# Loading x in 1 KB rows, writing the shuffle buffer in two parts and reading it in three: Fourier mixing and a three-way maxout layer on one Trainium2 core

## The chip, the core and the metric

The kernel runs on one core of a Trainium2 chip. The metric is the device time of one execution in microseconds (us). Five engines of the core take part, each with its own queue of instructions that it works through in order: PE (matmuls, with PEld for its weight loads), DVE (vector operations), ACT (activations and copies), POOL (table generation and the issue of some DMAs) and SP (the issue of other DMAs). Sixteen DMA engines move the data; SP's, ACT's and POOL's DMAs share them.

## What is computed

```python
X = np.fft.fft(np.fft.fft(x, axis=1), axis=2).real      # x: (8, 3072, 256), float32
t = X.reshape(24576, 256)
h = np.maximum(np.maximum(t @ w1, t @ w2), t @ w3)      # w1, w2, w3: (256, 768)
out = h @ w_out                                         # w_out: (768, 256)
```

## The kernel before

For each of the 8 batches the kernel first makes the Fourier mixing along the 3,072 rows, folded to its even and odd halves tE and tO ([128, 1536] each), and then runs the maxout layer on them. The transform along the 256 columns is folded into the weights once, at the start (gE, gO, gD, gw; `product`, `prep_first`, `prep_second`).

The mixing of one batch is done by class `Mix`, in steps that are called by letters in the plan:

- x is loaded by `load_x` as rows of 128 columns: row s of 96 in each of 32 blocks, with m the half of the columns, and h the block's front or its back, read from behind. Columns 0 to 127 go to partitions 0 to 63 of xt, columns 128 to 255 to partitions 64 to 127 of a second buffer xm. `mirror` (L125) and `mirror_first` (L129) copy that second half on DVE to xt in reversed order. Batch 0 is loaded by SP in float32 (x0) and cast by ACT and DVE; later batches are loaded by POOL, which casts to bfloat16.
- **s** (L349): a matmul over 128 partitions for 8 of the 49 rows s, copied to tb (s0 to s6).
- **y** (L363): tb is written to a buffer db in DRAM, in rows of 256 B.
- **z** (L370): db is read back as yb, with partitions and rows exchanged; four DMAs on SP.
- **x** (L377, L379): a small matmul for column 0 of x, which ACT copies straight into yb after z has landed.
- **k** (L388, L390): matmuls of yb with the tables te_tab and to_tab, for E and O and three groups g of 512 columns, copied to tE and tO by ACT. **end** (L395) does the middle row.

The maxout layer of a batch has 18 units (three blocks of six): `unit_plus` (L405, L406) gives one sign, ACT's relu (L419) and DVE's max (L420) take it to hp; `unit_minus` (L413) changes the accumulated sums to the other sign, which goes to hm. The second layer (`l2_block`: L429, L444, L452) follows one block later in pieces of ten between the units. Its sums become the tile ot on DVE (L457), which has six buffers; half of it is stored by SP (L469), half scattered by POOL (L462).

The order is written by hand. The dictionary `plan` says which steps of the next batch's mixing run in which unit: from batch 2 on, the s steps in units 1 to 4, y in 4, z in 6, x in 11, and the k steps in 12 to 17. `fetch` loads x of the batch after that in units 1, 3, 5 and 7, and `turn` mirrors it in 13 to 16. For mixings 1 and 2 the plan has lists of its own (`ahead0`, `ahead1`). Units above 17 lie in the next iteration.

Before the first unit the tables are made: POOL's iotas, DVE's range reduction, ACT's sines. The pool `gen` that holds them is closed ahead of the maxout layer, so that its space is used again by h_pool and others. load_w(0) waits for x's third chunk, load_w(1) for the first z. `warm_up` issues matmuls whose results are not used.

Of the kernel before, what the change touches and what calls it, by code (L numbers as in the profile page):

```python
# [9 lines left out]
FP32 = mybir.dt.float32  # L10
# [33 lines left out]
def kernel(  # L44
# [9 lines left out]
    nc = tc.nc  # L54
# [20 lines left out]
    xt = [consts.tile([128, 64 * 128], BF16, name=f"xt{i}", tag=f"xt{i}") for i in range(2)]  # L75
    xt = [t.rearrange("p (s f) -> p s f", f=128) for t in xt]
    xm_t = consts.tile([128, NS * 128], BF16, tag="xm")
    xm = xm_t.rearrange("p (s f) -> p s f", f=128)
    tb = consts.tile([128, 25 * 128], BF16, tag="tb")
    tbv = tb.rearrange("p (s f) -> p s f", f=128)  # L80
    yb = consts.tile([128, 2 * RI * 128], BF16, tag="yb")
    ybv = yb.rearrange("p (r e f) -> p r e f", e=2, f=128)
# [24 lines left out]
    def load_x(b, s0, s1, eng, dsts, after=None):  # L107

        rows = x[b].rearrange("(a s) (m f) -> m a s f", s=96, m=2)
        for m, dst in enumerate(dsts):  # L110
            if dst is None:
                continue
            for h in range(2):
                lo, hi = (s0, s1) if h == 0 else (max(s0, 1), min(s1, 48))
                src = rows[m]
                src = src[:, lo:hi, :] if h == 0 else src[:, 97 - hi:97 - lo, :][:, ::-1, :]
                p0 = 64 * m + 32 * h
                ld = eng.dma_start(out=dst[p0:p0 + 32, lo:hi, :], in_=src)
                if after is not None:
                    tc.add_manual_dep(ld.ins, after.ins.name, AFTER, reason="others first")  # L120
        return ld

    def mirror(b, s0, s1, src, fn):

        fn(out=xt[b % 2][64:128, s0:s1, 1:128], in_=src[64:128, s0:s1, 127:0:-1])  # L125

    def mirror_first(b, s0, s1, src, fn):

        fn(out=xt[b % 2][64:128, s0:s1, 0], in_=src[64:128, s0:s1, 0])  # L129

    gen_pool_cm = tc.tile_pool(name="gen", bufs=1)
    gen = gen_pool_cm.__enter__()
# [7 lines left out]
    FIRST = ((0, 16), (16, 32), (32, 40), (40, 49))  # L140
    x0_t = gen.tile([128, NS * 128], FP32, tag="x0")
    x0 = x0_t.rearrange("p (s f) -> p s f", f=128)
    for p0 in (32, 96):
        nc.vector.memset(x0[p0:p0 + 32, 0::48, :], 0.0)
    for c, (s0, s1) in enumerate(FIRST):
        ld = load_x(0, s0, s1, nc.sync, (x0, x0))
        if c == 2:
            third_chunk = ld
    nc.vector.memset(yb, 0.0)
    for i in range(2):  # L150
        nc.gpsimd.memset(xt[i][:, NS:64, 0], 0.0)
    nc.gpsimd.memset(xt[1][32:64, 0::48, :], 0.0)
    nc.gpsimd.memset(xm[96:128, 0::48, :], 0.0)
# [5 lines left out]
    iota(arv[:, :, 0:16], [[0, 4], [1, 16]], base=1)  # L159
    iota(arv[:, :, 16], [[0, 4]])  # L160
    dvec = gen.tile([128, 128], FP32, tag="dvec")
    iota(dvec, [[1, 128]])
    kvec = gen.tile([128, NHALF + 1], FP32, tag="kvec")
# [9 lines left out]

    half_pi = gen.tile([128, 1], FP32, tag="half_pi")
    nc.vector.memset(half_pi, 0.5 * math.pi)
    ang_o = gen.tile([128, 4 * RI], FP32, tag="ang_o")
# [36 lines left out]

    vm = gen.tile([128, 512], FP32, tag="vm")
# [18 lines left out]
    nc.scalar.activation(out=md_all, in_=vm, func=AX.Sin, scale=float(2.0 * math.pi / 256.0))  # L233
    nc.scalar.activation(out=nmd_all, in_=vm, func=AX.Sin, scale=float(-2.0 * math.pi / 256.0))

    act = nc.scalar.copy
    dve = nc.vector.tensor_copy

    def low_cast(s0, s1):
        act(out=xt[0][0:64, s0:s1, :], in_=x0[0:64, s0:s1, :])  # L240

# [16 lines left out]

    low_cast(*FIRST[0])
    mirror(0, *FIRST[0], x0, dve)  # L260
    mirror_first(0, *FIRST[0], x0, dve)
    angles(0, 512)
    low_cast(*FIRST[1])
    mirror(0, *FIRST[1], x0, dve)
    mirror_first(0, *FIRST[1], x0, dve)

# [10 lines left out]
    load_w(0, third_chunk)  # L277
# [3 lines left out]
    scal(dif, sgn, 1.0, ALU.subtract)  # L281

# [54 lines left out]
    class Mix:  # L337
# [7 lines left out]
        def s(self, k, pool=ps_f, evict=nc.scalar.copy):  # L345
            ps1 = pool.tile([128, 512], FP32, name="ps1", tag="ps")
            if k < 6:
                for hh in range(2):
                    nc.tensor.matmul(ps1, tab_at[hh], self.x[:, 8 * k + hh:8 * k + 8:2, :],  # L349
                                     start=(hh == 0), stop=(hh == 1))  # L350
                evict(out=tb[:, k * 512:(k + 1) * 512], in_=ps1)  # L351
            else:
                nc.tensor.matmul(ps1[:, 0:128], tab_at[0], self.x[:, 48, :],
                                 start=True, stop=True)
                evict(out=tbv[0:64, 24, :], in_=ps1[0:64, 0:128])

        def y(self, s0=0, s1=NS):
# [3 lines left out]
            for hh in range(2):  # L361
                n = (s1 - s0 + 1 - hh) // 2
                nc.sync.dma_start(out=dst[:, s0 + hh:s1:2, :],  # L363
                                  in_=tbv[hh * 64:hh * 64 + 64, s0 // 2:s0 // 2 + n, :])

        def z(self):
            for (a, z) in ((0, 48), (48, NS)):
                for cs in range(2):
                    q0, n = cs * 2 * RI * 128, (2 * RI - 4 * cs) * 128
                    last = nc.sync.dma_start(out=yb[cs * 64 + a:cs * 64 + z, 0:n],  # L370
                                             in_=self.db[a:z, q0:q0 + n])
            return last

        def x0(self, evict=nc.scalar.copy):
            psx = ps_f.tile([128, 512], FP32, name="psx", tag="ps")
            for cs in range(2):
                nc.tensor.matmul(psx[cs * 64:cs * 64 + 64, 0:RI], self.x[:, :, 0],  # L377
                                 tabx[:, cs * RI:(cs + 1) * RI], start=True, stop=True)
            evict(out=ybv[:, :, 1, 0], in_=psx[:, 0:RI])  # L379

        def k(self, which, g):

            special = {0: [(0, 0, 32)], 1: [(0, 0, 16), (16, 16, 16)], 2: [(16, 0, 32)]}[g]
            parts = special + [(5 * g + 1 + i, 32 + 96 * i, 96) for i in range(5)]
            tab = (te_tab, to_tab)[which]
            ps2 = ps_f.tile([128, 512], FP32, name="ps2", tag="ps")
            for (r, c0, wd) in parts:
                nc.tensor.matmul(ps2[:, c0:c0 + wd], ybv[:, (r - 1) % RI, which, :],  # L388
# [3 lines left out]
        def end(self):  # L392
            ps3 = ps_f.tile([128, 512], FP32, name="ps3", tag="ps")
            for which, tab in enumerate((te_tab, to_tab)):
                nc.tensor.matmul(ps3[:, which:which + 1], ybv[:, 16, which, :],  # L395
# [157 lines left out]
    warm_up(8)  # L553
    m.s(0, pool=ps_s, evict=dve)
    m.s(1, pool=ps_s)
    m.y(0, 16)
    warm_up(2)
    low_cast(*FIRST[2])
    mirror(0, *FIRST[2], x0, dve)
    mirror_first(0, *FIRST[2], x0, dve)  # L560
    m.s(2, pool=ps_s, evict=dve)
    m.s(3, pool=ps_s)
    m.y(16, 32)
    warm_up(2)
    low_cast(*FIRST[3])
    mirror(0, *FIRST[3], x0, dve)
    mirror_first(0, *FIRST[3], x0, dve)
    m.s(4, pool=ps_s, evict=dve)
    m.s(5, pool=ps_s)
    m.s(6, pool=ps_s, evict=dve)  # L570
    m.y(32, NS)
    y_first = m.z()
    tables(0, 512)
    angles(512, NHALF + 1)
    tables(512, NHALF + 1)

    for half in range(2):
        keep_product(product(0, half, 0, ps_f, "ps"), 0, half, 0, dve)
    for half in range(2):
        keep_product(product(1, half, 0, ps_s, "ps"), 1, half, 0, dve)  # L580
    m.x0()
    HALVES = ((0, 25), (25, NS))
    load_w(1, y_first)
    wld = nc.gpsimd.dma_start(out=wout_bf.rearrange("p (jc c) -> p jc c", jc=NJC),
                              in_=moe_w_out.rearrange("(jc p) c -> p jc c", jc=NJC))
    for (s0, s1) in HALVES:
        load_x(1, s0, s1, nc.gpsimd, (xt[1], xm))

    rows_f = gen.tile([128, 12 * B], FP32, tag="rows_f")
    rows_v = rows_f.rearrange("p (b r) -> p b r", r=12)  # L590
# [177 lines left out]
```

## Time and profile before

| | |
|---|---|
| median of 3 runs | 482.77 us (478.15 to 485.17) |
| the profiled execution | 484.2 us, of which 482.4 are the span of its instructions |
| mean granted clock of PE | 0.943 |
| iterations 2, 3, 4, 5 and 6, from end to end of a mixing (L395) | 52.78, 53.27, 54.61, 54.89, 47.45 us |
| PE's total wait for yb<-db in k (directly) | 18.5 us |
| DMA | 103,625 packets, 54.34 MB |

In the profile's rows a line begins with the engine and the line of the kernel; `out<-in` are tiles. Where a row ends in square brackets, they hold the time that the engine was idle ahead of it and what ended that. In the row of slices a digit is the busy share in tenths of a 40th of the span, or the granted share of PE's clock. "DMA share" is the mean busy share of the 16 DMA engines; it counts overlapping packets, so that it can exceed 1. A q behind an engine (SPq) marks its queue of DMA issues.

### The profile page before, as it was taken

The numbers are of one execution on the slowest core, as the hardware profiler recorded it, in microseconds if no ns is written. First come the engines' busy times: TensorE is split into PE (matmuls) and PEld (weight loads), VectorE is DVE, ScalarE is ACT, GpSimd is POOL, SyncE is SP. The second block draws the span as 40 slices with busy tenths as digits, with TensorE's granted clock in tenths as the row PEclk, the third lists the DMA queues.
The fourth block names the chain that finished last, engine by engine and source line by source line (L and its number), as shares of the span: only waits on it lengthen the run. The fifth ranks groups of instructions, "written<-read, shape, count | busy, mean of one in ns | idle before, by whom it ended". The sixth has DMA issues, their size and how long they took to land.

```text
span 482.4 us, 8139 instructions
## 1 busy us (share of the span) xinstructions
PE 417.0 (86%) x2756; PEld 254.5 (53%) x2756; DVE 296.2 (61%) x505; ACT 256.3 (53%) x470; POOL 172.9 (36%) x274
## 2 busy tenths in 40 slices
PE   0726979979984999799979999699969999999996
PEld 0312545546552666365646666365635656665665
DVE  6922784737553667385747666385736757667773
ACT  1741556546642765376535664366526665755550
POOL 3246134514450355133632456124621323222530
PEclk9966998989995999899998999799997999999999
DMA  9959316954594299625991399424981238222224
GB/s 164 182 110 169 33 19 92 237 100 86 79 190 104 69 134 167 137 76 89 179 173 48 82 144 168 107 84 78 177 171 42 84 83 176 64 78 67 74 67 123
DMA packets 103625, 54.34 MB, mean 113 GB/s; under 512 B 78600, under 2 KB 99856, under 8 KB 103192
## 3 DMA queue, kind: packets, MB, share of 16 engines
q0 software_dynamic: 54576, 24.70, 34.8%
q1 hardware_dynamic: 48848, 28.99, 27.1%
q8 instruction: 21, 0.34, 0.3%
q10 hardware_dynamic: 160, 0.13, 0.1%
q14 instruction: 20, 0.16, 0.1%
HBM read 34.73 MB, written 31.59 MB: 137 GB/s over the span
## 4 chain that ended last, share of the span: by engine, by line
PE 66%; DMA 23%; DVE 4%; ACT 3%; issue 2%; SPq 2%; POOL 1%; ACTq 0%; DVEq 0%
PE po L429 21%; DMA yb<-db 11%; PE pse L405 11%; PE pse L406 10%; PE pse L413 10%; DMA db<-tb 9%; PE ps L349 4%; PE po L452 3%; PE ps L388 2%; PE pl L444 2%; DMA wout_bf<-in_moe_w_out_dram 1%; DMA out_dram<-ot 1%; ACT stmp L419 1%; PE warm L550 1%; DVE hm L420 1%
## 5 line engine op out<-in xcount | busy, mean ns | idle before, releaser
L419 ACT ACTIVATE stmp<-pse 128x512 bf16<-128x512 f32 x288 | 169.8, 600 | 89.9 <-PE pse L406 69.5
L462 POOL DMA_INDIRECT out_dram<-ot,rows_m x92 | 107.5, 1168 | 268.6 <-DVE ot L457 249.5
L420 DVE TENSOR_TENSOR hp<-pse,stmp 128x512 bf16<-128x512 f32 x144 | 99.5, 691 | 137.9 <-ACT stmp L419 72.5
L405 PE MATMUL pse<-tE,gE 128*128 128x512 bf16 x288 | 112.3, 390 | 1.9 <-ACT stmp L419 1.3
L406 PE MATMUL pse<-tO,gO 128*128 128x512 bf16 x288 | 113.1, 393 | 0.1
L420 DVE TENSOR_TENSOR hm<-pse,stmp 128x512 bf16<-128x512 f32 x144 | 99.0, 688 | 11.4 <-ACT stmp L419 11.2
L413 PE MATMUL pse<-tO,gD 128*128 128x512 bf16 x288 | 88.7, 391 | 0.0
L429 PE MATMUL po<-wout_bf,hp 128*128 128x256 bf16 x576 | 87.3, 275 | 0.0
L429 PE MATMUL po<-wout_bf,hm 128*128 128x256 bf16 x576 | 81.2, 279 | 0.0
L429 PEld LDWEIGHTS <-hp 128*128 128x128 bf16 x576 | 57.0, 99 | 27.3 <-issue 1.1
L429 PEld LDWEIGHTS <-hm 128*128 128x128 bf16 x576 | 57.6, 100 | 18.7 <-issue 2.7
L457 DVE TENSOR_TENSOR ot<-po,even 128x512 f32<-128x512 f32 x92 | 62.8, 683 | 1.5 <-PE po L429 1.5
L413 PEld LDWEIGHTS <-gD 128*128 128x128 bf16 x288 | 28.3, 100 | 34.1 <-issue 3.2
L406 PEld LDWEIGHTS <-gO 128*128 128x128 bf16 x288 | 28.6, 99 | 26.4 <-issue 7.1
L405 PEld LDWEIGHTS <-gE 128*128 128x128 bf16 x288 | 28.7, 100 | 23.3 <-issue 2.6
L388 PE MATMUL ps<-te_tab,yb 128*128 128x96 bf16 (+2 forms) x152 | 11.6, 210 | 33.0 <-DMA yb<-db 18.5
L351 ACT CAST tb<-ps 128x512 bf16<-128x512 f32 x45 | 24.4, 588 | 25.1 <-PE ps L349 25.1
L388 PEld LDWEIGHTS <-yb 128*128 128x128 bf16 x304 | 17.7, 102 | 35.9 <-DMA yb<-db 28.5
L452 PE MATMUL po<-gw,tO 128*128 128x512 bf16 x92 | 36.0, 391 | 0.0
L349 PE MATMUL ps<-xt,tabz 128*128 128x512 bf16 x96 | 25.9, 390 | 4.2 <-DVE xt L129 2.4
L448 ACT COPY even<-pl 128x512 f32<-128x512 f32 x46 | 26.8, 583 | 0.8 <-PE pl L444 0.7
L379 ACT CAST yb<-psx 128x17 bf16<-128x17 f32 x8 | 1.9, 234 | 45.7 <-DMA yb<-db 30.2
(134 smaller groups left out, 271.3 us busy)
## 6 DMA issues: line engine op xcount, KB each, us to landing
out_dram<-ot SPq DMA_DIRECT2D x75, 96.0 KB, 1.9
yb<-db SPq DMA_DIRECT2D x8, 408.0 KB, 4.8
out_dram<-ot SPq DMA_DIRECT2D x48, 64.0 KB, 4.7
yb<-db SPq DMA_DIRECT2D x8, 360.0 KB
db<-tb SPq DMA_DIRECT2D x7, 400.0 KB, 7.7
xt<-in_x_dram POOLq DMA_DIRECT2D x14, 192.0 KB, 4.9
xm_t<-in_x_dram POOLq DMA_DIRECT2D x14, 192.0 KB, 8.6
db<-tb SPq DMA_DIRECT2D x7, 384.0 KB, 9.0
```

What stands on the lines that cost most here:

```text
L349: nc.tensor.matmul(ps1, tab_at[hh], self.x[:, 8 * k + hh:8 * k + 8:2, :], start=(hh == 0), stop=(hh == 1))
L388: nc.tensor.matmul(ps2[:, c0:c0 + wd], ybv[:, (r - 1) % RI, which, :], tab[:, g * 512 + c0:g * 512 + c0 + wd], start=True, stop=True)
L405: nc.tensor.matmul(pse[:, 0:n], gE[i][:, js], te, start=True, stop=False)
L406: nc.tensor.matmul(pse[:, 0:n], gO[i][:, js], to, start=False, stop=True)
L413: nc.tensor.matmul(pse, gD[i][:, js], to, start=False, stop=True, skip_group_check=True)
L419: nc.scalar.activation(out=stmp[:, 0:n], in_=pses[0][:, 0:n], func=AX.Relu)
L420: nc.vector.tensor_tensor(out=dst, in0=src3, in1=stmp[:, 0:n], op=ALU.max)
L429: nc.tensor.matmul(po, hcols(jc), wout_bf[:, jc * 256:(jc + 1) * 256], start=False, stop=(jc == NJC - 1), skip_group_check=True)
L448: nc.scalar.copy(out=even, in_=pl)
L452: nc.tensor.matmul(po, to[:, cp], gw[:, 256:768], start=True, stop=True)
L457: nc.vector.tensor_tensor(out=ot.rearrange("p (h c) -> p h c", h=2), in0=po.rearrange("p (h c) -> p h c", h=2), in1=lin.unsqueeze(1).to_br ...
L462: stored(nc.gpsimd.indirect_dma_start(out, bass.IndirectOffsetOnAxis(ap=rows_m[0:128 - lo, b * 12 + slot: b * 12 + slot + 1], axis=0), ot[ ...
```

## The change

- x is loaded as whole rows of 256 columns (1 KB in DRAM) to partitions 0 to 63 of a wider xt; DVE's mirror copies columns 255 to 129 from there to partitions 64 to 127, and the first column (128) with each chunk. The buffer xm is gone. Batch 0 is loaded in the same way by POOL, cast on the way; ACT's and DVE's casts are gone.
- y is in two parts, rows 0 to 23 after s2 and the rest after s6. z is in three parts of four DMAs, one for each group of k; the order of the rows in yb and in the tables' angles is changed to fit. At the start the last write's two DMAs are issued by SP and ACT.
- The small matmul for column 0 goes to a tile x0s without waiting for z; a copy c, on POOL (ACT for a part of batch 0), takes it from there into yb.
- The pool `gen` stays open to the end. rows_m is made earlier.
- The tables are made in three parts, the last in unit 0; warm-up matmuls are placed elsewhere (4, 8 and 12 in place of 8, 2 and 2); no product is made before unit 0; load_w(0) no longer waits, and load_w(1) waits for the first third of z.
- The plan: z in unit 7, c in 11, k in 13 to 17, x loads in 9 to 12, mirrors in 14 to 17; the two special lists alike.

```diff
+    def load_x(b, s0, s1, h):
+        rows = x[b].rearrange("(a s) d -> a s d", s=96)
+        lo, hi = (s0, s1) if h == 0 else (max(s0, 1), min(s1, 48))
+        src = rows[:, lo:hi, :] if h == 0 else rows[:, 97 - hi:97 - lo, :][:, ::-1, :]
+        return nc.gpsimd.dma_start(out=xt[b % 2][32 * h:32 * h + 32, lo:hi, :], in_=src)
+    def mirror(b, s0, s1):
+        t = xt[b % 2]
+        nc.vector.tensor_copy(out=t[64:128, s0:s1, 1:128], in_=t[0:64, s0:s1, 255:128:-1])
+        nc.vector.tensor_copy(out=t[64:128, s0:s1, 0], in_=t[0:64, s0:s1, 128])
-    gen_pool_cm = tc.tile_pool(name="gen", bufs=1)
+    gen = ctx.enter_context(tc.tile_pool(name="gen", bufs=1))
...
+        def z(self, parts=(0, 1, 2), engs=(nc.sync, nc.sync)):
+            spans = {0: ((0, 6, 0), (1, 6, 17)), 1: ((6, 12, 6), (6, 11, 22)),
+                     2: ((12, 17, 12), (12, 17, 27))}
+            for part in parts:
+                for cs in range(2):
+                    (i0, i1, c0) = spans[part][cs]
+                    c1 = c0 + i1 - i0
+                    for (a, z) in ((48, NS), (0, 48)):
+                        done.append(engs[cs].dma_start(
+                            out=yb[cs * 64 + a:cs * 64 + z, i0 * 256:i1 * 256],
+                            in_=self.db[a:z, c0 * 256:c1 * 256]))
...
-            evict(out=ybv[:, :, 1, 0], in_=psx[:, 0:RI])
+                nc.scalar.copy(out=x0s[cs * 64:cs * 64 + NS, :],
+                               in_=psx[cs * 64:cs * 64 + NS, 0:RI])
+        def c(self, i0=0, i1=RI, fn=nc.gpsimd.tensor_copy):
+            fn(out=ybv[:, i0:i1, 1, 0], in_=x0s[:, i0:i1])
...
+    for (u, fn) in ((0, lambda: tables(1024, NHALF + 1)), (0, lambda: m.c(6, RI)),
+                    (1, prep_some), (2, prep_some), (2, prep_some), (2, prep_some),
+                    (3, lambda: m.k(0, 1)), (3, prep_some), (4, lambda: m.k(1, 1)),
+                    (4, prep_some), (5, prep_some), (5, prep_some),
+                    (7, lambda: m.k(0, 2)), (8, lambda: m.k(1, 2)), (8, m.end)):
...
-        at(0, (6, 7, 8, 9)[ch], lambda ch=ch: turn(1, ch))
-        at(0, (10, 11, 13, 15)[ch], lambda ch=ch: fetch(2, ch))
+        at(0, (7, 8, 10, 11)[ch], lambda ch=ch: turn(1, ch))
+        at(0, (12, 13, 14, 15)[ch], lambda ch=ch: fetch(2, ch))
...
-            at(b - 2, (1, 3, 5, 7)[ch] + (4 if b == 3 else 0), lambda b=b, ch=ch: fetch(b, ch))
-            at(b - 2, (13, 14, 15, 16)[ch], lambda b=b, ch=ch: turn(b, ch))
+            at(b - 2, (9, 10, 11, 12)[ch], lambda b=b, ch=ch: fetch(b, ch))
+            at(b - 2, (14, 15, 16, 17)[ch], lambda b=b, ch=ch: turn(b, ch))
-    ahead0 = {9: ("s0", "s1"), 10: ("s2", "s3"), 11: ("s4", "s5"), 12: ("s6", "y"), 13: ("z",),
-              17: ("x", "kE0", "kO0"), 20: ("kE1", "kO1"), 24: ("kE2",), 25: ("kO2", "end")}
-    ahead1 = {5: ("s0", "s1"), 6: ("s2", "s3"), 7: ("s4", "s5"), 8: ("s6", "y"), 9: ("z",),
-              14: ("x", "kE0"), 15: ("kO0", "kE1"), 16: ("kO1", "kE2"), 17: ("kO2", "end")}
-    ahead = {1: ("s0", "s1"), 2: ("s2", "s3"), 3: ("s4", "s5"), 4: ("s6", "y"),
-             6: ("z",), 11: ("x",), 12: ("kE0",), 13: ("kO0",), 14: ("kE1",), 15: ("kO1",),
-             16: ("kE2",), 17: ("kO2", "end")}
+    late = {13: ("kE0",), 14: ("kO0", "kE1"), 15: ("kO1",), 16: ("kE2",), 17: ("kO2", "end")}
+    ahead0 = {8: ("s0", "s1"), 9: ("s2", "y0"), 11: ("s3", "s4"), 12: ("s5", "s6", "y1", "x"),
+              13: ("z",), 16: ("c",), 17: ("kE0", "kO0"), 20: ("kE1",), 21: ("kO1",),
+              24: ("kE2",), 25: ("kO2", "end")}
+    ahead1 = {3: ("s0", "s1"), 4: ("s2", "y0", "s3"), 5: ("s4", "s5"), 6: ("s6", "y1", "x"),
+              9: ("z",), 12: ("c",), **late}
+    ahead = {1: ("s0", "s1"), 2: ("s2", "y0", "s3"), 3: ("s4", "s5"), 4: ("s6", "y1", "x"),
+             7: ("z",), 11: ("c",), **late}
```

## The prediction

> **What bounds the kernel now.** I read the page's busy times first, then its row of slices, to see whether one engine is full and where it is not.
>
> ```profile
> PE 417.0 (86%) x2756; PEld 254.5 (53%) x2756; DVE 296.2 (61%) x505; ACT 256.3 (53%) x470; POOL 172.9 (36%) x274
> PE   0726979979984999799979999699969999999996
> PEclk9966998989995999899998999799997999999999
> DMA  9959316954594299625991399424981238222224
> ```
>
> PE is the engine to fill: 417.0 us of 482.4. It is full in the last third and has a dent about every 53 us before that, with DMA digits near 9 just ahead of each dent. Second view, the waits, all engines, to see what those 65 idle us wait for:
>
> ```profile
> ACT yb L379 <- DMA yb<-db: 30.2, 5, 10.0
> ...
> PE ps L388 <- DMA yb<-db: 18.5, 6, 8.2
> ...
> PE ps L388 <- ACT yb L379: 11.2, 3, 4.4
> ...
> PE psg L289 <- DMA w_bf<-in_moe_w_dram: 5.0, 2, 4.2
> ...
> PE ps L349 <- DVE xt L129: 2.4, 1, 2.4
> ```
>
> The dents are the read of the shuffled buffer (yb<-db): the k step's matmuls wait for it, directly or through the small copy L379, which stands in ACT's queue. Third view, the stretches between two ends of a mix (L395): iterations 2, 5 and 6 of the loop over batches (columns: us, then busy us and count of PE, PEld, DVE, ACT, POOL; clock; DMA share; GB/s).
>
> ```profile
> 162.02:214.80 52.78, 49.17 (x335) 30.33 (x333) 33.69 (x55) 30.24 (x57) 21.11 (x32) 0.97 0.67 121
> ...
> 322.68:377.57 54.89, 50.20 (x336) 30.75 (x334) 33.62 (x55) 30.23 (x57) 21.04 (x32) 0.94 0.63 117
> 377.57:425.02 47.45, 47.45 (x336) 29.90 (x333) 31.08 (x50) 30.48 (x57) 14.28 (x24) 1.00 0.43 103
> ```
>
> Iteration 6 does the same PE work (336 matmuls), loads no x, and takes 47.45 us with PE busy throughout. So it is a measured model of an iteration without the wait. The timeline tells what differs (write L363, read L370, copy L379, of iterations 4 and 6):
>
> ```profile
> 284.75 3.52 SPq L363 DMA_DIRECT2D db<-tb  x2
> ...
> 294.58 1.48 SPq L370 DMA_DIRECT2D yb<-db  x2
> ...
> 305.89 0.23 ACT L379 CAST yb<-psx 128x17 bf16<-128x17 f32 x1 [7.02 <-DMA out_dram<-ot]
> ...
> 306.17 0.66 PE L388 MATMUL ps<-te_tab,yb 128*128 128x32 bf16 x6 [3.89 <-ACT yb L379]
> ...
> 394.25 1.70 SPq L363 DMA_DIRECT2D db<-tb  x2
> ...
> 401.39 1.39 SPq L370 DMA_DIRECT2D yb<-db  x4
> ...
> 409.33 0.23 ACT L379 CAST yb<-psx 128x17 bf16<-128x17 f32 x1 [0.96 <-PE psx L377]
> ```
>
> In iteration 4 two x loads are issued at 284.87 and two at 293.61, beside write and read; 21.1 us pass from the write's issue to the copy, in iteration 6 at most 15. PE idles 3.89 us and restarts with 512-column matmuls of 0.60 instead of 0.38 us, so a dent costs more than its idle time. Last, the start:
>
> ```profile
> 32.97 0.21 PE L388 MATMUL ps<-te_tab,yb 128*128 128x32 bf16 x1 [6.00 <-DMA yb<-db]
> ...
> 42.73 0.73 POOL L118 DMA_DIRECT2D xm_t<-in_x_dram  x1 [1.05 <-DMA wout_bf<-in_moe_w_out_dram]
> ...
> 44.58 0.60 ACT L419 ACTIVATE stmp<-pse 128x512 bf16<-128x512 f32 x1 [9.24 <-POOL rows_f L137]
> ```
>
> The first relu waits until 44.58, since its tile lies where the table pool was and rows_f, last of that pool, stands on POOL behind all of batch 1's x loads.
>
> **The change part by part.** All is summed against the profiled execution: 484.2 us, span 482.4 and 1.8 around it. It lies 1.4 above the median 482.77.
>
> *x in 1 KB rows.* 6,144 rows of 512 B per batch become 3,072 of 1 KB. No row shows this load. Nearest: at 430 to 470 us only 1 KB stores run, DMA share 0.24 at 69 GB/s, which is 0.24 x 16 / 67.4 rows per us = 57 ns a row and engine; 512 B rows at 0 to 10 us (0.96, 158 GB/s) take 50 ns. A batch's x costs 3,072 x 57 / 16 = 10.9 us of all engines, at most twice 50, which is the 19 us of now. I take 11, from the row of equal size. Issues on POOL go from eight to four a batch (0.78 us each), hidden in POOL's idle time.
>
> *Mirror.* Same elements, 0.56 us for 64x1524, now from partitions 0-63 to 64-127: no row shows DVE shifting partitions. Lower bound 0.56, upper the rate of the two-tensor fp32 add (0.69 us for 512, 1.23 for 1,025, so 1.75 for 1,524): +1.2 us x 4 a batch on a DVE with 14 us to spare per iteration; I take 0.56. The first column costs three copies more, under 0.28 each (L129). Both lie under PE's work; without that cover they would cost at most 5.5 us an iteration.
>
> *Write in two, read in three.* SP issues two writes more (0.7 each) and eight reads more (0.31 each): 4 us an iteration. Behind them in SP's queue stand only stores, whose six buffers cover half an iteration. POOL's last x load at the start waited for the load eight before it, so I expect a ninth read to wait for the first; that delays the last third, needed last. SP already shows 25.3 us of stores waiting for yb<-db at no visible cost.
>
> *Order.* From batch 2 on: first write after s2, second at unit 4, read at unit 7 (was 6), E matmuls at 13 (was 12), x loads at 9 to 12 (were 1 to 7), mirrors at 14 to 17. Write and read then meet only stores, as in iteration 6: read issued 7.1 us after the write, landed within 7.6 more. From unit 7 to 13 there are about 6 x 2.4 = 14 us. The small copy leaves ACT: psx goes to x0s without waiting, and the column copy c waits on POOL at unit 11, behind it one x load and scatters. kE0 already waited for the copy's write, so it will wait for c; c needs all twelve reads, 9.6 us after the first. Fits. Iterations 2 to 5: 52.78 + 53.27 + 54.61 + 54.89 - 4 x 47.45 = 25.8 us; x loads and mirrors remain in them, so I take 25 (bounds 12 and 25.8).
>
> *Iteration 1.* From psx to the mix's end 19.54 us pass for three units and all k groups; iteration 6 does six units with them in 16.04, so three fewer at 2.24 make 9.3. Excess 10.2 (8.25 idle, the rest low clock; its write took 15.8 us among x loads). x now follows the read; I take 9.5 (5 to 10.2).
>
> *Iteration 0.* Gone: PE's 2.4 us wait for a mirror and 3.1 (2.36 and 0.76) for the read. New: s1 stands in the same unit as its mirror chunk, s4 too (about 1.2 each); three products in unit 2 instead of spread (0 to 2, I take 0.6); the read still meets batch 2's x loads, units 12 to 15 (I take 2 of the 3.1). 5.5 - 2.4 - 0.6 - 2 = 0.5 (-4 to 5).
>
> *Start.* Gone: 16 loads on SP, ACT's casts (1.9 us for 64x2048), the wait for rows_f. Added on POOL ahead of its tables: eight loads, 6.2 us. The last write is issued near 24 us, as now: rows_m's dozen small DVE operations (0.15 each) come ahead of the last mirror, ACT's casts go. Its DMAs are small, and the first third of the read lands some 2 us before the whole (33.0). But 24 warm-up matmuls (12 now) and tables up to 1,024 lie before it, so I count no gain to k. After k, PE did about 3.7 us of use between 35.3 and 44.94 (one product, one unit, half a product), so 6 were lost; those go. Tables of the last 513 columns (3.2 us for 1,025, so 1.6) now press on ACT in unit 0: -1, the rest under PE's work. Warm clock: +0.5. Sum 5.5 (-1 to 10).
>
> *On the page's other side.* The trace has a mirror against a POOL scatter: 1.95 us where 0.56 is usual, the scatter 2.68 where 1.04 is:
>
> ```profile
> 66.16 2.68 POOL L462 DMA_INDIRECT out_dram<-ot,rows_m  x1 [14.93 <-DVE xt L125]
> ...
> 67.25 1.95 DVE L125 COPY xt<-xm_t 64x1524 bf16<-64x1524 bf16 x1
> ```
>
> If the eight first loads, now on POOL, suffer likewise (2.6 instead of 0.78 us), they take 21 us, the last chunk's s6 comes near 27 instead of 23, and the start loses 4 where I count +5.5. The Trainium skill (SBUF — State Buffer, "SBUF: two separate sides") speaks for this: POOL writes the descriptors of its loads through a port that two-port DVE instructions lock. By that rule the start is A below; the pair above agrees with it.
>
> Sum: 25 + 9.5 + 0.5 + 5.5 = 40.5; 484.2 - 40.5 = 443.7, less the 1.4: 442.3, say 442.
>
> **The rivals.** *A, the start is not shorter* (above): start -4, else as forecast: 484.2 - 31 - 1.4 = 452. For it: that pair, and a POOL order in which kvec's tables and the weights stand behind x. Against: but for one memset of 1.87 us, DVE's early instructions are short (0.06 to 0.5).
>
> *B, half of the wait stays.* Twelve reads in one queue, c behind POOL's scatters (each waiting for ot), E matmuls behind c: if c runs after unit 13, PE waits as now. Half of 25 + 9.5 kept, start as forecast: 442 + 17 = 459, up to 473 if the start fails too (9.5) and iteration 0 loses 4. For it: L379's waits of 6 to 10 us. Against: iteration 6.
>
> *C, slower: the mirrors wait for x.* Fetched at units 9 to 12, used from 14; the last chunk's load has four units, about 11 us. The mirror stands in DVE's in-order queue; behind it hp and hm, then PE. Slowest class of x load now: 13.5 us to landing. Five iterations fetch so; the gain of 40.5 is eaten when each waits 8.1 us, a landing 19 us after issue. At 22 it is 5 x 11 = 55 lost: 497. For it: all x now goes to 64 partitions, at the busiest point behind the read. Against: half as many rows, and x loads of partitions 0-63 landed in 4 to 5.5 us, those of 64-127 in 6 to 13.5. The Trainium skill (SBUF — State Buffer, "Door 1: The DMA port swizzle") says partitions 0-63 reach half the DMA ports that 0-127 reach, about 218 GB/s; as an estimate from that page, 1.57 MB of bf16 then needs 7.2 us, below the 11 from rows, so it would not bind. No run here shows it alone.
>
> **How the numbers follow.** Forecast 0.62, own range 432 (all upper bounds: 25.8 + 10.2 + 5 + 10 = 51) to 454. A 0.16, B 0.14, C 0.08. About 2% (9.7 us) is what a measurement of this kernel can tell from no change. Faster by over 2% (under 473): forecast, A, most of B: 0.88; within 2%: 0.05; slower: 0.07. Range 430 to 466: it takes in A and B's middle, leaves out B's end and C.
>
> **What would show it.** Right: stretches between mix ends near 47.5 us in iterations 2 to 5, no L388 wait for yb or c above 1 us, clock 1.00 there; first relu near 36 us. Wrong: DVE idle before the mirror with the x load as releaser (C), POOL's c waiting past unit 13 (B), first s6 past 25 us (A). A mirror row above 1 us would put the bound on DVE.

## The result and the profile after

The changed kernel takes 450.88 us (median of 4 runs, 450.28 to 454.19); the kernel before, beside it, 483.97 (478.15 to 487.45). The ratio is 0.937, interval 0.927 to 0.947: faster. The forecast, 442, is 8.9 us too low; its range (430 to 466) holds the time. The medians in this document are over all runs of a kernel, while the ratios leave out the runs that came out in a slower state of the chip: five of e5's ten, one of e3's four, and two of the thirteen of the kernel before beside e5 and e7 to e9. The profiled execution took 451.0 us with a span of 449.2, 33.2 less than the span of before.

The page of the kernel after, busy times and slices:

```profile
PE 406.6 (91%) x2768; PEld 250.8 (56%) x2768; DVE 296.1 (66%) x527; ACT 255.2 (57%) x481; POOL 155.1 (35%) x263
...
PE   1488889599987999999998999999999999999994
...
PEclk9999999869998999999999999999999999999999
DMA  7849246912496236943397257924693354312323
```

PE's row is 8 or 9 from slice 14 to the last but one; the dents that are left after the start lie in slices 8 and 13 (11.2 us each, so near 85 and 140 us: iterations 0 and 1). PE is busy for 406.6 instead of 417.0 us for 12 instructions more: PEclk, at 5 to 8 around each dent before, now stays at 9 behind slice 13. The stretches of the kernel after between two ends of a mix say the same (iterations 1, 2, 4 and 6; columns as in the prediction):

```profile
117.95:150.01 32.06, 27.40 (x199) 17.04 (x196) 19.52 (x33) 16.46 (x30) 12.33 (x19) 0.95 0.62 133
150.01:198.16 48.15, 47.59 (x337) 29.88 (x334) 33.47 (x56) 30.53 (x58) 17.60 (x29) 1.00 0.59 132
...
247.24:295.11 47.87, 47.57 (x336) 29.87 (x333) 33.73 (x57) 30.52 (x58) 17.56 (x29) 1.00 0.60 134
...
342.81:390.23 47.42, 47.42 (x336) 29.89 (x333) 32.09 (x52) 30.52 (x58) 14.44 (x25) 1.00 0.38 103
```

Set against the terms of the sum, from the ends of the mixes in both traces:

| part | before | after | gained | predicted |
|---|---|---|---|---|
| start and iteration 0 (to the second mix's end) | 123.94 | 117.95 | 6.0 | 5.5 + 0.5 |
| iteration 1 | 38.08 | 32.06 | 6.0 | 9.5 |
| iterations 2 to 5 | 215.55 | 192.80 | 22.75 | 25 |
| iteration 6 | 47.45 | 47.42 | 0 | 0 |
| rest, after the last mix | 57.38 | 58.97 | -1.6 | 0 |

The column of gains adds up to 33.2. The waits of the k step that are left stand in iterations 0 (2.71 and 3.53 us) and 1 (1.30 and 3.36). The timeline of the kernel after at the k step of iteration 1 (start, duration, instruction; in brackets the engine's idle time and what ended it):

```profile
133.76 0.40 PE L395 MATMUL ps<-te_tab,yb 128*128 128x96 bf16 x6 [1.30 <-DMA yb<-db]
...
139.61 0.26 POOL L385 COPY yb<-x0s 128x17 bf16<-128x17 bf16 x1 [8.84 <-DMA out_dram<-ot]
139.92 0.40 PE L395 MATMUL ps<-to_tab,yb 128*128 128x96 bf16 x6 [3.36 <-POOL yb L385]
```

Two things are to be seen. kE0 (te_tab) runs at 133.76, six us before the column copy c (L385): it does not wait for c, against what the prediction says. kO0 (to_tab) does; by the code c writes only the half of yb that kO0 reads. And c itself stood on POOL for 8.84 us. The line puts that down to a store of ot, but c reads no ot; what it needs, by the code, is the read.

### The profile page after: what moved, and what is told of

It is laid out like the page before. It is cut to its first block, busy times and chain, and to the rows that moved or that the text cites. A ratio compares the mean times of both kernels' runs of the same rounds, so it can differ in the third digit from the quotient of the medians.

```text
span 449.2 us, 8328 instructions
## 1 busy us (share of the span) xinstructions
PE 406.6 (91%) x2768; PEld 250.8 (56%) x2768; DVE 296.1 (66%) x527; ACT 255.2 (57%) x481; POOL 155.1 (35%) x263
## 3 DMA queue, kind: packets, MB, share of 16 engines
q0 software_dynamic: 23856, 26.28, 29.7%
## 4 chain that ended last, share of the span: by engine, by line
PE 70%; DMA 11%; DVE 7%; issue 4%; ACT 3%; SPq 2%; POOL 1%; DVEq 0%; ACTq 0%; POOLq 0%
PE po L436 22%; PE pse L412 12%; PE pse L420 11%; PE pse L413 11%; DMA yb<-db 5%; PE ps L344 5%; PE po L459 3%; DMA xt<-in_x_dram 3%; DMA out_dram<-ot 3%; ACT stmp L426 2%; DVE hm L427 2%; PE pl L451 2%; PE ps L395 2%; SPq L476 1%; DVE ot L464 1%
## 5 line engine op out<-in xcount | busy, mean ns | idle before, releaser
L469 POOL DMA_INDIRECT out_dram<-ot,rows_m x92 | 105.4, 1146 | 234.2 <-DVE ot L464 219.2
L412 PE MATMUL pse<-tE,gE 128*128 128x512 bf16 x288 | 110.0, 382 | 3.1 <-DVE hm L427 2.4
L413 PE MATMUL pse<-tO,gO 128*128 128x512 bf16 x288 | 110.0, 382 | 0.1
L420 PE MATMUL pse<-tO,gD 128*128 128x512 bf16 x288 | 86.6, 382 | 0.0
L436 PE MATMUL po<-wout_bf,hm 128*128 128x256 bf16 x576 | 78.6, 273 | 0.0
L344 PE MATMUL ps<-xt,tabz 128*128 128x512 bf16 x96 | 27.5, 403 | 18.7 <-DVE xt L117 17.8
L346 ACT CAST tb<-ps 128x512 bf16<-128x512 f32 x47 | 25.9, 588 | 30.5 <-PE ps L344 30.5
L397 ACT CAST tO<-ps 128x512 bf16<-128x512 f32 x24 | 14.1, 586 | 24.0 <-PE ps L395 12.9
L116 DVE COPY xt<-xt 64x1524 bf16<-64x1524 bf16 (+4 forms) x32 | 19.1, 596 | 9.4 <-DMA xt<-in_x_dram 5.6
L397 ACT CAST tE<-ps 128x512 bf16<-128x512 f32 x24 | 14.1, 587 | 19.4 <-PE ps L395 19.4
```

The lines of the kernel that those rows point to most:

```text
L397: nc.scalar.copy(out=(self.tE, self.tO)[which][:, g * 512:(g + 1) * 512], in_=ps2)
L412: nc.tensor.matmul(pse[:, 0:n], gE[i][:, js], te, start=True, stop=False)
L413: nc.tensor.matmul(pse[:, 0:n], gO[i][:, js], to, start=False, stop=True)
L420: nc.tensor.matmul(pse, gD[i][:, js], to, start=False, stop=True, skip_group_check=True)
L436: nc.tensor.matmul(po, hcols(jc), wout_bf[:, jc * 256:(jc + 1) * 256], start=False, stop=(jc == NJC - 1), skip_group_check=True)
L469: stored(nc.gpsimd.indirect_dma_start(out, bass.IndirectOffsetOnAxis(ap=rows_m[0:128 - lo, b * 12 + slot: b * 12 + slot + 1], axis=0), ot[ ...
```

## The experiments

Twelve kernels were run. The prediction's reason, theory 1 in what follows, is the place of the x loads: they were beside write and read, and now stand behind the read. Its rivals: that the copy for column 0 left ACT's queue (4a where the theories are split), that the read was cut into parts, that the rows are longer. Iterations are measured from mix end to mix end; iteration 0 starts at the end of the first mix, and their lengths are those of the one profiled execution of each kernel. They carry noise: e6, whose edit lies ahead of unit 0, differs from the kernel before by 3.9 us in iterations 2 to 5 (211.64 to 215.55), so differences of that size in the last column say nothing. By 2%, e5, e6 and e8 are the same as the kernel before, e10 is unclear, and the others are faster.

| label | median | ratio to before, interval | iterations 0; 1; 2 to 5 together |
|---|---|---|---|
| kernel after | 450.88 | 0.937 (0.927-0.947) | 61.19; 32.06; 192.80 |
| e1_x_early | 446.62 | 0.922 (0.917-0.926) | 58.71; 29.50; 192.14 |
| e2_read_whole | 446.45 | 0.921 (0.917-0.925) | 57.28; 29.99; 190.40 |
| e3_x_behind_0_1 | 440.33 | 0.908 (0.903-0.913) | 52.56; 28.72; 194.02 |
| e4_half_rows | 451.63 | 0.933 (0.928-0.937) | 58.48; 31.08; 193.14 |
| e5_before_order | 485.33 | 0.994 (0.989-1.000) | 63.05; 39.87; 212.09 |
| e7_early_half_rows | 446.81 | 0.923 (0.916-0.929) | 60.26; 31.38; 190.76 |
| e8_early_c_on_act | 477.23 | 0.987 (0.981-0.994) | 58.88; 34.02; 214.26 |
| e9_behind_whole | 437.85 | 0.903 (0.897-0.909) | 52.87; 30.13; 190.70 |
| e10_before_c_pool | 479.78 | 0.987 (0.980-0.994) | 59.84; 39.36; 206.63 |
| e11_before_c_pool_k13 | 465.97 | 0.958 (0.951-0.965) | 60.07; 39.97; 194.51 |
| e6_before_rows | 479.54 | 0.988 (0.980-0.995) | 60.47; 38.20; 211.64 |
| e12_start | 435.76 | 0.897 (0.890-0.903) | 52.56; 30.21; 190.55 |

### The first four: one part of the change undone, or carried further

**e1_x_early**: the kernel after, its x loads at the units of before.

```diff
-        at(0, (12, 13, 14, 15)[ch], lambda ch=ch: fetch(2, ch))
+        at(0, (10, 11, 13, 15)[ch], lambda ch=ch: fetch(2, ch))
...
-            at(b - 2, (9, 10, 11, 12)[ch], lambda b=b, ch=ch: fetch(b, ch))
+            at(b - 2, (1, 3, 5, 7)[ch] + (4 if b == 3 else 0), lambda b=b, ch=ch: fetch(b, ch))
```

> The changed kernel with the x loads put back to their old units (1, 3, 5, 7; 5, 7, 9, 11 for batch 3; 10, 11, 13, 15 for batch 2), all else as changed. Theory 1 (the old dents came from x loads beside the write and the read, and the new order takes them away): dents return in iterations 2 to 5, which go from 48.2 us in the mean to 50 to 52, and the time from 451 to 459 to 467; less than before the change, since x now has half as many rows. Theory 2 (splitting the read and taking the small copy off ACT removed the dents, the order of x does not matter): within 3 us of 451.

No dent came back in iterations 2 to 5: they take 192.14 us, 0.7 less than in the kernel after, and the whole is 4.3 us faster, a little below what theory 2 allowed and far from the 459 to 467 of theory 1. x stands beside write and read again, and the read lands late again: in these iterations c stands 5.2 to 7.1 us for it on POOL, against 0.9, 6.2, 1.7 and 1.3 us in the kernel after. The copy c in iteration 4, of the kernel after and then of e1 (the releasers named are again not what c needs):

```profile
281.70 0.26 POOL L385 COPY yb<-x0s 128x17 bf16<-128x17 bf16 x1 [1.74 <-ACT even L455]
...
279.65 0.26 POOL L385 COPY yb<-x0s 128x17 bf16<-128x17 bf16 x1 [5.38 <-DMA out_dram<-ot]
```

PE does not notice. So the new order does bring the read forward, but the dents stay away without it. In iteration 1 the kernel after is even slower than this one (32.06 to 29.50): there x now stands at units 9 to 12 and the read at 9.

**e2_read_whole**: the kernel after, each read in six DMAs over the whole range instead of twelve.

```diff
-            for part in parts:
-                for cs in range(2):
-                    (i0, i1, c0) = spans[part][cs]
...
+            for (cs, i0, i1, c0) in ((0, 0, 17, 0), (1, 1, 11, 17), (1, 12, 17, 27)):
+                c1 = c0 + i1 - i0
```

> The changed kernel with the read in six DMAs of whole ranges in place of twelve in three parts; the write stays in two. Theory 1 (the dents left in iterations 0 and 1 are x loads beside the read): these dents stay at 2 to 4 us each, kE0 waits longer at the start and in iteration 0 since no first third lands early: 451 to 455. Theory 3 (they come from twelve reads in a queue that lets only eight be under way, so that the last ones and the column copy come late): the dents shrink, 445 to 448.

The cut into thirds does not carry the gain: without it iterations 3 to 5 take 47.42 us each, as iteration 6, and in iterations 2 to 5 c finds the read landed, where it stood up to 6.2 us in the kernel after. This is what theory 3 said of twelve reads. Only batch 0 loses by it: its k waits until 34.72 us instead of 30.91, and mix 0 ends 4.0 us later. The later iterations win that back and 4.4 us more.

**e3_x_behind_0_1**: the kernel after, x of batch 2 at units 15 to 18 of iteration 0 and of batch 3 at 11 to 14 of iteration 1, its mirrors one unit later.

```diff
-        at(0, (12, 13, 14, 15)[ch], lambda ch=ch: fetch(2, ch))
+        at(0, (15, 16, 17, 18)[ch], lambda ch=ch: fetch(2, ch))
...
-            at(b - 2, (9, 10, 11, 12)[ch], lambda b=b, ch=ch: fetch(b, ch))
-            at(b - 2, (14, 15, 16, 17)[ch], lambda b=b, ch=ch: turn(b, ch))
+            at(b - 2, (9, 10, 11, 12)[ch] + (2 if b == 3 else 0), lambda b=b, ch=ch: fetch(b, ch))
+            at(b - 2, (14, 15, 16, 17)[ch] + (1 if b == 3 else 0), lambda b=b, ch=ch: turn(b, ch))
```

> The changed kernel with batch 2's x loads at units 15 to 18 of iteration 0 (was 12 to 15), batch 3's at 11 to 14 of iteration 1 (was 9 to 12) and batch 3's mirrors one unit later. Theory 1 (x beside the read makes the dents left in iterations 0 and 1, 6.2 and 4.7 us of idle PE and the low clock behind them): they go, 439 to 444. Theory 3 (twelve reads through eight places): they stay, 449 to 453. If the mirrors of batches 2 and 3 now wait for x, PE idles before s0 and the time is above 451.

10.6 us by the medians, and iterations 0 and 1 are 8.6 and 3.3 shorter. Here the order does count: in these two iterations the kernel after issues x at the read's own units, close ahead of the read's use. The timeline of this kernel at the first k step of iteration 0, where the kernel after waits 2.71 us for the read and 3.53 for c:

```profile
83.21 0.39 PE L395 MATMUL ps<-te_tab,yb 128*128 128x96 bf16 x6
...
83.90 0.26 POOL L385 COPY yb<-x0s 128x17 bf16<-128x17 bf16 x1 [0.17 <-DMA yb<-db]
...
84.22 0.40 PE L395 MATMUL ps<-to_tab,yb 128*128 128x96 bf16 x6 [0.62 <-POOL yb L385]
84.38 0.54 POOL L111 DMA_DIRECT2D xt<-in_x_dram  x1 [0.22 <-issue]
```

The last x load is issued behind c, and PE's idle time ahead of kO0 falls to 0.62 us. In iteration 1 waits of 1.23 and 1.77 us stay.

**e4_half_rows**: the kernel after, each x load cut into two of 128 columns (512 B rows).

```diff
-        return nc.gpsimd.dma_start(out=xt[b % 2][32 * h:32 * h + 32, lo:hi, :], in_=src)
+        for m in (0, 128):
+            ld = nc.gpsimd.dma_start(out=xt[b % 2][32 * h:32 * h + 32, lo:hi, m:m + 128],
+                                     in_=src[:, :, m:m + 128])
+        return ld
```

> The changed kernel with each x load as two DMAs of 128 columns, 512 B rows in place of 1 KB, to the same partitions. If the row size carries part of the gain: x takes 19 us of the DMA engines instead of 11, mirrors at units 14 to 17 wait 2 to 5 us in iterations 1 to 5, and batch 0's start is 2 to 4 us later: 458 to 475. If only the order carries it: within 4 us of 451.

451.63 against 450.88: the row length is worth nothing that can be seen in the time. Mix 0 ends 2.9 us later (59.69 to 56.76), and iterations 0 and 1 give 3.7 back.

### What made the dents

**e8_early_c_on_act** changes one thing in e1: c of batches 1 to 7 runs on ACT, as the copy did before, and not on POOL.

```diff
-        def c(self, i0=0, i1=RI, fn=nc.gpsimd.tensor_copy):
+        def c(self, i0=0, i1=RI, fn=nc.scalar.copy):
...
-    for (u, fn) in ((0, lambda: tables(1024, NHALF + 1)), (0, lambda: m.c(6, RI)),
+    for (u, fn) in ((0, lambda: tables(1024, NHALF + 1)), (0, lambda: m.c(6, RI, nc.gpsimd.tensor_copy)),
```

> The changed kernel with early x loads, and the column copy c of batches 1 to 7 on ACT in place of POOL, at the same units. With early loads POOL's c waited about 5 us for the read. Theory 4a (the wait in ACT's queue made the dents, since relus stand behind it): ACT waits 4 to 5 us per iteration, PE idles 2 to 4 us and runs at the low clock behind it, 460 to 475. Theory 4b (only k's own wait for yb counts): 445 to 449.

477.23 against 446.62: 30.6 of the 37.8 us by which e1 beats the kernel before, for the place of a copy of 0.27 us, and 2.2 above the range expected for theory 4a. Iterations 2 to 5 are 22.1 us longer. The timeline of this kernel in iteration 4:

```profile
284.97 1.24 ACT L426 ACTIVATE stmp<-pse 128x512 bf16<-128x512 f32 x2 [1.14 <-PE pse L413]
...
289.00 0.10 PEld L412 LDWEIGHTS <-gE 128*128 128x128 bf16 x1
291.40 0.27 ACT L385 COPY yb<-x0s 128x17 bf16<-128x17 bf16 x1 [5.19 <-DMA out_dram<-ot]
291.51 1.08 ACT L426 ACTIVATE stmp<-pse 128x512 bf16<-128x512 f32 x2
292.13 0.69 DVE L427 TENSOR_TENSOR hp<-pse,stmp 128x512 bf16<-128x512 f32 x1 [4.52 <-ACT stmp L426]
292.48 0.59 ACT L455 COPY even<-pl 128x512 f32<-128x512 f32 x1
292.64 0.58 PE L412 MATMUL pse<-tE,gE 128*128 128x512 bf16 x1 [3.37 <-ACT stmp L426]
```

The copy holds ACT from 286.2 to 291.4; the relu (stmp) of a unit that needs nothing of it stands behind it, then hp, then the buffer pse that PE needs. PE waits 3.37 us and restarts with matmuls of 0.58 instead of 0.38. The wait is as long on POOL (5.38 us in e1), but no relu stands behind it there.

**e5_before_order** is the reverse: the kernel before, its x loads at the units of the kernel after.

```diff
-            at(b - 2, (1, 3, 5, 7)[ch] + (4 if b == 3 else 0), lambda b=b, ch=ch: fetch(b, ch))
-            at(b - 2, (13, 14, 15, 16)[ch], lambda b=b, ch=ch: turn(b, ch))
+            at(b - 2, (9, 10, 11, 12)[ch], lambda b=b, ch=ch: fetch(b, ch))
+            at(b - 2, (14, 15, 16, 17)[ch], lambda b=b, ch=ch: turn(b, ch))
```

> The kernel before, with nothing but x's place changed: x loads at units 9 to 12 (12 to 15 in iteration 0), mirrors at 14 to 17. Theory 4 (what counts is whether the read lands before ACT and PE come to it; taking x out of its way is one sufficient cure, the later k steps, the copy off ACT and the read in parts are others): iterations 2 to 5 fall from 53.9 to 48 to 51 us, 462 to 472 in all, some of it lost again to mirrors that wait for x in 512 B rows. If the place of x does nothing: 481 to 487.

No gain that 2% would tell (0.994), and the 462 to 472 of theory 4 were missed. Its profiled execution, 488.5 us, is near the top of its ten runs (478.2 to 490.5), so I read from it only where the waits are. The waits for the read are gone from PE in iterations 2 to 5, and ACT's copy stands 0.96 to 2.76 us there instead of 6.0 to 7.5. Others stand in their place, 2.56 to 5.03 us each. The timeline of this kernel in iteration 2:

```profile
208.66 0.68 DVE L420 TENSOR_TENSOR hm<-pse,stmp 128x512 bf16<-128x512 f32 x1
...
214.25 0.62 DVE L125 COPY xt<-xm_t 64x1651 bf16<-64x1651 bf16 x1 [4.91 <-DMA xm_t<-in_x_dram]
214.90 0.69 DVE L420 TENSOR_TENSOR hp<-pse,stmp 128x512 bf16<-128x512 f32 x1
...
216.24 0.58 PE L405 MATMUL pse<-tE,gE 128*128 128x512 bf16 x1 [3.62 <-DVE hm L420]
```

DVE stands 4.91 us before a mirror whose x has not landed, and PE waits for the hm behind it. This is the mechanism of rival C, in the kernel before. So x's place does delay the read, but moving x alone moves the stall to another in-order queue. The run is not quite the change's order: in the kernel before the half of x that is mirrored is loaded last, at units 11 and 12, while in the kernel after the first two mirrors need only the loads of units 9 and 10.

**e10_before_c_pool** is the kernel before with only the copy moved: psx goes to x0s by ACT in the unit of the write, and c runs on POOL (at unit 11 from batch 2 on; on ACT for batch 0). **e11_before_c_pool_k13** moves kE0 and kO0 one unit later as well, from batch 2 on.

```diff
-            evict(out=ybv[:, :, 1, 0], in_=psx[:, 0:RI])
+            evict(out=x0s, in_=psx[:, 0:RI])
+
+        def c(self, fn=nc.gpsimd.tensor_copy):
+            fn(out=ybv[:, :, 1, 0], in_=x0s)
...
+    ahead = {1: ("s0", "s1"), 2: ("s2", "s3"), 3: ("s4", "s5"), 4: ("s6", "y", "x"),
+             6: ("z",), 11: ("c",), 12: ("kE0",), 13: ("kO0",), 14: ("kE1",), 15: ("kO1",),
```

and in e11, against e10, also

```diff
-             6: ("z",), 11: ("c",), 12: ("kE0",), 13: ("kO0",), 14: ("kE1",), 15: ("kO1",),
+             6: ("z",), 11: ("c",), 13: ("kE0",), 14: ("kO0", "kE1"), 15: ("kO1",),
```

> The kernel before with one thing changed: the small matmul's result goes to a tile of its own at the unit of the write (4 from batch 2 on), and POOL copies it into yb at unit 11, so that no instruction of ACT waits for the read. x, write, read and k as before. Theory 4a says ACT's waits of 6 to 10 us go; but kE0, at unit 12, still needs the whole read, which landed about 3 us after its turn: half of the dents stay, iterations 2 to 5 at 50 to 52.5 us, 468 to 478. If ACT's wait was all: 458 to 463. If the read's lateness was all: 481 to 486.

> The same, and from batch 2 on the k steps one unit later, as in the changed kernel (kE0 at 13, kO0 and kE1 at 14, kO1 at 15). Both together should put every use behind the landing: iterations 2 to 5 at 47.5 to 49.5 us, 458 to 467. If 1 KB rows, the split write or the split read are needed too: above 470.

e10 misses its expectation: 5.1 us instead of 7 to 17. In iterations 2 to 5 it gains 8.9, but the first mix ends 2.3 us later. At unit 12 kE0 still waits 1.1 to 1.7 us for the read, in three of the four iterations once more 0.5 to 1.2 us within it, and PE is busy for 2 us an iteration more than at full clock. kE0 and c of this kernel in iteration 2:

```profile
202.03 0.19 PE L392 MATMUL ps<-te_tab,yb 128*128 128x32 bf16 x1 [1.74 <-DMA yb<-db]
...
203.33 0.26 POOL L383 COPY yb<-x0s 128x17 bf16<-128x17 bf16 x1 [5.78 <-DMA yb<-db]
```

One unit more and nearly all of that is gone: e11 takes 194.51 us for iterations 2 to 5, 21.0 of the 22.75 gained by the whole change. Two of its stretches, iterations 3 and 5 of e11:

```profile
215.39:262.99 47.60, 47.60 (x336) 29.94 (x333) 33.52 (x54) 30.43 (x57) 21.59 (x33) 1.00 0.79 134
...
312.64:361.17 48.53, 47.85 (x335) 30.00 (x333) 33.54 (x54) 30.24 (x57) 21.37 (x33) 1.00 0.71 132
```

PE is full at full clock, or nearly (iterations 2 and 4 take 48.73 and 49.65 us), with x in 512 B rows, beside write and read as before, the write and the read not split. The DMA engines are busier than in the kernel after (0.71 to 0.79 against some 0.60), and it does not matter. The later k with the copy left on ACT was not run in the kernel before; e8 is nearly that, and shows no gain in these iterations (214.26 us).

**e7_early_half_rows**: e1 with the halved rows of e4 (the same edit). It asks whether the two parts cover for each other.

> The changed kernel with the x loads at their old units and in 512 B rows too, so that x stands beside write and read just as before the change. Theory 4: the other parts still move the read's landing ahead of its use, no dent above 2 us in iterations 2 to 5, 446 to 454. If the smaller number of rows is what kept the kernel with early x loads free of dents: they return with 2 to 4 us each, 457 to 468.

446.81 against 446.62 in e1: they do not. Once the copy is off ACT and k late, neither x's place nor its row length is worth anything that can be seen in iterations 2 to 5.

### The start, and a version that beats both

**e6_before_rows**: the kernel before, with the block that makes rows_f and rows_m placed ahead of the loads of the second weights and x of batch 1.

```diff
-    load_w(1, y_first)
...
-    for (s0, s1) in HALVES:
-        load_x(1, s0, s1, nc.gpsimd, (xt[1], xm))
...
+    load_w(1, y_first)
...
+    for (s0, s1) in HALVES:
+        load_x(1, s0, s1, nc.gpsimd, (xt[1], xm))
```

> The kernel before with rows_f and rows_m made ahead of the second weights' and batch 1's loads, so that the first relu no longer waits for POOL's issue queue. The profile put 9.24 us of ACT's wait on rows_f, but the product in front of unit 0 (PE until 39.8) and the second weights stand ahead too: first relu at 41 to 42.5 in place of 44.58, 481 to 483. If the wait on rows_f was all: 476 to 478.

479.54, ratio 0.988: 5.4 us, more than the 481 to 483 expected, and less than 2%. The first relu starts at 42.19 instead of 44.58, and mix 0 ends 1.65 us earlier, mix 1 only 0.6. The other 3.9 us of the profiled execution lie in iterations 2 to 5, which the edit does not touch. So rows_f behind x's loads was a price of some 2 us in the start, a small part of the 11.7 us by which the change brings the first relu forward (to 32.88).

**e9_behind_whole** puts e3 together with e2's six-DMA reads, batch 0 alone still in thirds. **e12_start** adds to e9 the second mirror of batch 0 ahead of the reduction of vm, and the third ahead of the operations for rows_m, on DVE.

```diff
+        def z_whole(self):
+            for (cs, i0, i1, c0) in ((0, 0, 17, 0), (1, 1, 11, 17), (1, 12, 17, 27)):
...
-            mm.z()
+            mm.z_whole()
```

and in e12 also

```diff
+    mirror(0, *FIRST[1])
...
-    mirror(0, *FIRST[1])
+    mirror(0, *FIRST[2])
...
-    mirror(0, *FIRST[2])
```

> Two finds together: x of batches 2 and 3 behind the read (as in the run at 440.3), and the read of batches 1 to 7 in six DMAs of whole ranges, batch 0's still in three parts. If the small waits left in iterations 2 to 5 (0.5 to 1.4 us each) come from c standing late in POOL's queue ahead of an x load, they go, and the time falls to 435 to 438; if the thirds are needed for kE0, its wait grows in iterations 0 and 1 and the time is 441 to 445.

> The best kernel so far (437.85) with batch 0's second mirror ahead of the range reduction of vm and the third ahead of rows_m's operations, so that the s matmuls, which waited 5.7 us for the second mirror, come earlier. The last write should be issued near 22.2 us in place of 24.4 and the first k near 29: 435 to 436.5. If x's second chunk lands too late or ACT's sines come in the way of the evictions: 437 to 440.

e9 takes 437.85 us; its interval overlaps that of e3, so what the six reads add there is not told apart. Its iterations 3 to 6 all take 47.42 us. In e12 the second chunk's s2 starts at 13.09 us (17.53 in the kernel after, where PE waited 5.70 us for its mirror), mix 0 ends 2.5 us earlier than in e9, and the time is 435.76 us, ratio 0.897 (0.890 to 0.903): the best of all, 15 us under the kernel after.

## Why the prediction was right, and where not

**Iterations 2 to 5: the size right, the cause half right.** 22.75 us of 25, inside 12 to 25.8. The step that failed is "Order". It reads the dent as x loads beside write and read, and lets the copy's move to POOL pass in a subordinate clause, with "kE0 already waited for the copy's write, so it will wait for c". In the kernel after kE0 runs before c. That x's place delays the read holds (the waits of the copy in e1 and e5). But x may stand beside the read (e1) without a dent. Put the copy back on ACT there, and iterations 2 to 5 take 22.1 us more (e8). Take it off ACT and put k one unit later in the kernel before, and 21.0 go, with x's order as it was (e11); the copy alone brings 8.9 (e10). So the change holds two cures at once: a read that lands earlier, and nothing on PE's way that stands behind a late read. The second is enough by itself. Whether the first is enough with the copy left on ACT, no run shows, since in e5 the mirrors stall.

The line that tells it was on show: "ACT yb L379 <- DMA yb<-db: 30.2, 5, 10.0". It covers the start and iterations 0 to 3. I took it as a wait for the read on the way to k. It was ACT standing, with all its later work behind it: in iterations 2 to 5 the copy stood 6.45, 6.01, 7.02 and 7.53 us, the last two put down to stores. PE's idle time then lies ahead of kE0 (3.33, 2.89, 3.89 and 4.41 us), and not, as in e8, ahead of a unit. Whether kE0 waited there for the copy itself or for the buffer of ps_f that psx held until ACT had copied it was not tried apart; that kE0 runs ahead of c in the kernel after and in e10 speaks for the buffer. The comparison with iteration 6 gave the right size because it measures what any cure of the dent can bring, whatever the cause.

**Iteration 1: 9.5 predicted, 6.0 measured.** "x now follows the read" does not hold there: the loads start at unit 9, the read is issued at 9. 1.30 and 3.36 us of waits stay (first timeline above). With x two units later the iteration takes 28.72, 9.4 less than before (e3): the size of the term was that of the cure, not of the change.

**Iteration 0 and start: 6.0 in sum, as predicted, by luck: two errors cancel.** Mix 0 ends 7.8 us earlier (64.54 to 56.76), though its end stands one unit later in the plan, and iteration 0 takes 1.8 us longer (59.40 to 61.19). "I take 2 of the 3.1" was too little: the read met batch 2's loads and cost 2.71 + 3.53 = 6.2 us (e3 takes 8.6 us off this iteration). The start, sized at 5.5, brought more. k comes 2.1 us earlier (30.91 to 32.97), where I counted no gain. The first relu follows k by 1.97 instead of 11.61 us. Of these 9.6 at most the 3.7 us that PE used before are still to be done, so by this estimate the start gained at least 8 (its upper bound was 10). Of the many edits in the start only rows_f was tried alone (e6). One of them is smaller than the list of changes says: both kernels make four products ahead of unit 0, and only a fifth went behind it.

**The rest after the last mix** is 1.6 us longer, which no term had. PE's work in it takes 52.7 us in both; SP's last 14 stores take 8.30 instead of 6.70 us of issue. The same goes for all the kernels: the stretch takes 57.4 to 57.5 us where this issue takes 6.7 (the kernel before and its variants, e9 and e12), 58.4 where it takes 7.7 (e3), and 58.9 to 59.4 where it takes 8.2 to 8.7. What makes the issue longer stays open.

Together the misses are 2.25 + 3.5 + 1.6 = 7.35 us of span; the remaining 1.5 are the 1.4 that I took off for the profiled execution of before, and rounding. The upper end of the forecast's own range, 454, is not worked out from the terms: their lower bounds add up to 12 us, which gives 471.

**The rivals.** *A* fell, though the time, 450.88, is next to its 452: POOL issued the eight first loads in 4.76 us (2.89 to 7.65), no slower than the 0.78 each of before, and the last chunk's s5 and s6 came at 23.19 and 23.62, under the 25 named. The rule of the Trainium skill (SBUF — State Buffer, "SBUF: two separate sides") that POOL cannot write descriptors while a two-port DVE instruction holds the shared port cost nothing here, where DVE's instructions took 0.07 to 0.28 us but for one memset of 1.87; a mirror beside a scatter still agrees with it (2.82 us for a scatter at 55.04, the mirror 1.39 beside it). *B* happened in iterations 0 and 1 only, by its own mechanism: c late on POOL, kO0 behind it. *C* did not: the mirrors wait 5.6 us for x in all (4 waits, the longest 2.0) and once 2.9 us that the profile puts down to nothing, and cost PE 0.56 and 1.27 us, in iterations 2 and 3. e5 shows that its mechanism is real with the loads of the kernel before. The estimate from the Trainium skill (SBUF — State Buffer, "Door 1: The DMA port swizzle"), that 64 partitions would not bind, agrees with these short waits, though no run here puts this x on 128 partitions. *The mirror* costs 0.55 to 0.62 us from partitions 0-63 to 64-127, as taken. *The queue*: reads wait for earlier reads in SP's queue, six times, as expected; the page of waits of the kernel after has it:

```profile
SPq L370 <- DMA yb<-db: 10.8, 6, 5.1
```

*The rows*: e4 against the kernel after, queue 0 takes 40.1% instead of 29.7% of 16 engines' span, (0.401 x 448.7 - 0.297 x 449.2) / 8 = 5.8 us of all engines per batch; I had 8. The time is the same (451.63 to 450.88), as the prediction, which gives the rows no gain of their own, has it.

The single write of y instead of two was not tried alone; e11 keeps the single write and has 21.0 of the 22.75.

## What to carry to other kernels

Ask of every instruction that waits for a DMA what stands behind it on its engine, and price that, not the instruction: here a copy of 0.27 us cost 30 us on ACT, where relus stood behind it, and far less on POOL, where in the kernel after it held up only kO0 of iterations 0 and 1 (3.5 and 3.4 us). A comparison with an iteration that lacks the wait gives the size of the gain, not its cause; a wait line that names the busy engine's in-order queue is worth one experiment of its own. When a change holds two cures of one wait, undoing one shows only that it is not needed; put each alone into the kernel before as well. When a transfer is moved out of another's way, look at the iterations with a plan of their own too: in the first two x still met the read, and moving it two or three units on was worth 10.6 us.

## What the runs showed that I had not expected

- Busy DMA engines were no bound here: iteration 3 of e11 ran at 47.60 us with the DMA engines at 0.79 of their time, and iterations 2 to 5 of e8 at 51 to 55 us with them at 0.53 to 0.58.
- A stall can cost PE more than its length: in iterations 4 and 5 of e8, with stalls of 3.37 and 5.63 us, the granted clock is 0.94, and PE's busy time 50.24 and 49.65 us for the work that takes 47.42 at full clock. In iteration 2, with a stall of 3.17 us, the clock stays at 1.00 and PE is busy for 47.74 us.
- Halving x's packets freed 5.8 us of all DMA engines per batch and changed the time by 0.75 us, within the noise of the runs.
